# First two experts: the last 128 slots as a tile of their own, 448 columns and 64 rows behind a branch

## The chip, the cores and the metric

One core of a Trainium2 chip runs the whole kernel. Its engines have instruction streams of their own and wait for each other by semaphores: TensorE (PE in the profile; PEld is its weight loads) multiplies and transposes, VectorE (DVE) and ScalarE (ACT) work on tiles, GpSimd (POOL) issues the gathers and scatters here, and SyncE (SP) issues the other DMAs. The metric is the device time of one execution in microseconds, the median of several; the profile comes from one further execution.

## The reference

A linear attention with a complex decay gives x, and a mixture of eight experts follows. What matters here is the second part (x is 3072 tokens of 384, w1 is 8 x 384 x 1024, w2 is 8 x 1024 x 384):

```python
logits = x @ w_gate
noisy_logits = logits + np.log1p(np.exp(x @ w_noise)) * noise
top2 = np.argpartition(-noisy_logits, 2, axis=1)[:, :2]
...                                   # softmax over the two: top2_w
for e in range(E):
    for k in range(2):
        mask = top2[:, k] == e
        h = np.maximum(x[mask] @ w1[e], 0.0)
        out[mask] += top2_w[mask, k, None] * (h @ w2[e])
```

Each token goes to two of the eight experts, so an expert gets 768 tokens on average, some more and some fewer.

## The kernel before

The first 260 us compute the attention and the gates; a planner's table (ORDER) sets their order. Each token's row, with its gate weights and its number, is scattered to a slot of its expert in `xs`; an expert has 832 slots (CAP) that are computed, and two windows: window 0 and window 1. For the first two experts (not in TAILS) window 0 is slots 0 to 319 and window 1 is slots 320 to 831, both computed in full. For experts 2 to 7 (TAILS) window 1 is 512 slots, and window 0 is 256 slots and a tail of 64, slots 768 to 831.

For each window, SyncE loads its rows (`load_x`, into the single buffers `xga` for window 0 and `xgb` for window 1). `x_T` transposes them on TensorE, three blocks of 128 model columns (kk), each into one of two PSUM buffers `px`; ScalarE rounds each block to the high half and VectorE takes the low half. `mm1` makes eight groups of nine products (three blocks times high/high, high/low, low/high) of all the window's columns, each group into a buffer `ph`; ScalarE applies the Relu (`h`), VectorE takes the low half of `h`. `mm2_tile` then makes one tile of 128 slots from 24 products of 384 columns in `po`; for a tile of 64 slots it places the low half of `h` beside the high half as further rows and makes 16 products, and ScalarE and VectorE add the two halves of the result. VectorE scales the tile by the gate weight and adds it to the gathered rows `ao`, and GpSimd scatters them to `out`. The weights are split the same way as they arrive (`load_w1`, `load_w2`, a ring of three buffers `raw`).

Experts 2 to 7 branch already: `mm1_tail` loads a flag from `tail` (is the expert's count above 768?) on TensorE, VectorE, ScalarE and GpSimd. The long side runs window 0 with 320 columns and the 64-row tile, the short side with 256 columns and without that tile. SyncE doesn't take part.

The program's text from `mm2(0, 0)` on gives the work of the experts in the order in which it is written; the scheduler puts an engine's instructions in an order of their readiness, but what stands behind a branch in the text stays behind it on the engines that take it, apart from work that hangs on no instruction of the branch, which it may put ahead.

Of the kernel before, what the change touches and what calls it, by code (L numbers as in the profile page):

```python
# [9 lines left out]
F32 = mybir.dt.float32  # L10
# [3 lines left out]
I32 = mybir.dt.int32  # L14
# [63 lines left out]
def kernel(  # L78
# [460 lines left out]
    def load_x(e, w, dst):  # L539
        if w == 0:  # L540
            t = CAP - 64 if e in TAILS else 256
            ds = [nc.sync.dma_start(dst[:, 0:2], x3[e, 0:256].rearrange("(p j) r -> p j r", j=2)),
                  nc.sync.dma_start(dst[0:64, 2], x3[e, t:t + 64])]
            if e == 1:

                for d in ds:
                    for s in late:
                        tc.declare_no_dep(d.ins, s.ins, reason="slots behind the first 320")
        else:
            o = 256 if e in TAILS else 320  # L550
            nc.sync.dma_start(dst, x3[e, o:o + 512].rearrange("(p j) r -> p j r", j=4))

# [88 lines left out]
    def mm1_group(e, w, f, h, c):  # L643
        n = WIN[w][1]
        t = n % 128
        p = ps_tile("ph", 4)
        ms = [(i, j, kk) for kk in range(KD) for i, j in ((0, 0), (0, 1), (1, 0))]
        for m, (i, j, kk) in enumerate(ms):
            LAST['m'] = nc.tensor.matmul(p[:, :c], W1[e, kk][i][:, f * 128:(f + 1) * 128], XW[w, kk][:, j, 0:c],  # L649
                                         start=(m == 0), stop=(m == len(ms) - 1))  # L650
        nc.scalar.activation(h[:, 0:c], p[:, :c], AF.Relu)  # L651
        for dst, a, b in ((n + t, 0, n - t), (n, n - t, n)):
            b = min(b, c)
            if a < b:
                LAST['h'] = nc.vector.scalar_tensor_tensor(h[:, dst:dst + b - a], p[:, a:b], 0.0, h[:, a:b].bitcast(F32),  # L655
                                                           op0=OP.max, op1=OP.subtract)

    def mm1_tail(e):
# [8 lines left out]
        with cmp.Else():  # L667
            for f in range(KF):
                mm1_group(e, 0, f, hs[f], n - n % 128)

    def gather_o(e):
        for j in (2, 3, 4, 5, 6, 0, 1) if e in TAILS else range(7):
            w = TW[j]
            nc.gpsimd.indirect_dma_start(  # L674
                out=ao[j][0:w, :], out_offset=None, in_=out,
                in_offset=bass.IndirectOffsetOnAxis(ap=OX[e][0:w, j:j + 1], axis=0),
                bounds_check=N - 1, oob_is_err=False)
# [4 lines left out]

    def mm2(e, w):
        for j in JS[w]:
            if TW[j] == 128 or e not in TAILS:
                mm2_tile(e, w, j)

    def po_tile():
        return psO.tile([128, 512], F32, name="po")

    def mm2_tile(e, w, j, p=None):
        n, o = TW[j], 128 * (j - JS[w][0])
        p = p or po_tile()
        a, g = ao[j][0:n, :], GW[e][0:n, j:j + 1]
        if n == 128:
            ms = [(f, i, k2) for f in range(KF) for i, k2 in ((0, 0), (0, 1), (1, 0))]
            for m, (f, i, k2) in enumerate(ms):
                LAST['po'] = key(f"PO.{e}.{j}", nc.tensor.matmul(p[:, :DM], HT[w, f][i][:, o:o + 128], W2[f // 2][k2][:, f % 2, :],  # L698
                                                start=(m == 0), stop=(m == len(ms) - 1)))
        else:  # L700

            for f in range(KF):
                for k2 in range(2):
                    nc.tensor.matmul(p[0:2 * n, :DM], HT[w, f][0][:, o:o + 2 * n], W2[f // 2][k2][:, f % 2, :],  # L704
                                     start=(f == 0 and k2 == 0), stop=(f == KF - 1 and k2 == 1))
            lo = mt([n, DM], F32, name="lo")
            nc.scalar.copy(lo, p[n:2 * n, :DM])
            nc.vector.scalar_tensor_tensor(a, lo, g, a, op0=OP.mult, op1=OP.add)
        nc.vector.scalar_tensor_tensor(a, p[0:n, :DM], g, a, op0=OP.mult, op1=OP.add)  # L709
        d = nc.gpsimd.indirect_dma_start(  # L710
            out=out, out_offset=bass.IndirectOffsetOnAxis(ap=OX[e][0:n, j:j + 1], axis=0),
            in_=a, in_offset=None, bounds_check=N - 1, oob_is_err=False)
        if n == 128 and e in TAILS:

            for s in DONE.setdefault(e, []):
                tc.declare_no_dep(d.ins, s.ins, reason="rows differ")
            DONE[e].append(d)
# [125 lines left out]
    mm1(1, 0)  # L843
    x_T(0, 1)
    load_x(2, 0, xga)
    mm1(0, 1)
    load_x(1, 1, xgb)
    load_w1(2)
    mm2(0, 1)
# [1 line left out]

    lim = mp.tile([128, E], F32, name="lim")
    nc.gpsimd.iota(lim, pattern=[[N, E]], base=CAP, channel_multiplier=0, allow_small_or_imprecise_dtypes=True)

    for m in HALVES:
        nc.vector.tensor_add(bad[:, 0, 2 * m:2 * m + 1], bad[:, 0, 2 * m:2 * m + 1], bad[:, 0, 2 * m + 1:2 * m + 2])
# [1 line left out]
    nc.vector.tensor_scalar(decm, decm, DEC_MIN, None, op0=OP.is_lt)  # L860
    nc.vector.tensor_reduce(bad[0:112, 0, 1:2], decm[0:112], axis=AX.X, op=OP.max)
    nc.vector.tensor_scalar(bad[:, 1], bad[:, 1], TAN_MAX ** 2, None, op0=OP.is_gt)
    tail = cp.tile([1, E], I32, name="tail")
    nc.vector.scalar_tensor_tensor(tail, lim[0:1], -64.0, base_run[0:1], op0=OP.add, op1=OP.is_lt)
    few = mp.tile([128, E], F32, name="few")
    nc.vector.scalar_tensor_tensor(few, lim, float(FILL - CAP), base_run, op0=OP.add, op1=OP.is_gt)
    nc.vector.tensor_tensor(lim, base_run, lim, op=OP.is_gt)
# [13 lines left out]

    load_w2(1)
    gather_o(1)
    mm1(1, 1)
    load_x(2, 1, xgb)
    mm2(1, 1)
    x_T(2, 1)
# [185 lines left out]
```

## Time and profile before

| | |
|---|---|
| median of 3 runs | 709.2 us (709.17, 709.2, 710.77) |
| the profiled execution's own time | 710.01 us |
| its span | 708.3 us |
| mean granted clock of TensorE | 0.991 |
| busy in the span: PE, DVE, ACT, POOL | 94%, 58%, 46%, 24% |

The profile shows one execution. Its span is the time from the first to the last instruction; busy shares are over that span. A start time in a row is counted from the span's start. "Idle before" is how long an engine had nothing to do, and the arrow names what released it. The granted clock is a share of TensorE's full 2.4 GHz.

### The profile page before, as it was taken

How to read it: one execution, taken by the hardware profiler on the slowest of the kernel's cores; microseconds unless marked ns; L12 is line 12 of the kernel's file. 1: busy time of each engine (PE TensorE's matmuls, PEld its weight loads, DVE VectorE, ACT ScalarE, POOL GpSimd, SP SyncE). 2: the span in 40 equal slices, each digit the busy share in tenths (PEclk: the TensorE clock that was granted, in tenths of full speed). 3: DMA queues.
4: the chain of work that ended last, by engine and by line, in shares of the span. 5: the costliest groups of instructions: out<-in, count | busy, mean ns of one | idle time of the engine just before them, and what ended most of it. 6: DMA issues, size and time to landing. Idle time of an engine off the chain costs nothing.

```text
span 708.3 us, 13293 instructions
## 1 busy us (share of the span) xinstructions
PE 666.2 (94%) x5120; PEld 590.7 (83%) x5120; DVE 411.2 (58%) x919; ACT 328.0 (46%) x553; POOL 172.6 (24%) x183
## 2 busy tenths in 40 slices
PE   2599999999998999999999999999999999999995
PEld 0388887887776889898998998998999899899995
DVE  6799899999988747545237325425524524524311
ACT  7699888888775542324125215215313413413300
POOL 3000012451404225113224122322321411411311
PEclk9989999999999999999999999999999999999998
DMA  8877863654238516325128125425415515502201
GB/s 315 255 217 211 268 181 127 174 200 131 94 92 277 178 72 249 130 84 187 59 80 264 30 91 169 129 90 169 132 40 175 179 37 178 173 23 68 65 33 36
DMA packets 64190, 100.24 MB, mean 142 GB/s; under 512 B 26296, under 2 KB 46533, under 8 KB 64112
## 3 DMA queue, kind: packets, MB, share of 16 engines
q1 hardware_dynamic: 54752, 71.68, 32.7%
q0 software_dynamic: 9360, 27.54, 11.0%
q8 instruction: 46, 0.75, 0.4%
q14 instruction: 32, 0.26, 0.1%
HBM read 68.55 MB, written 31.69 MB: 142 GB/s over the span
## 4 chain that ended last, share of the span: by engine, by line
PE 80%; DVE 8%; ACT 5%; DMA 4%; issue 1%; SPq 1%; another core or an unknown queue 0%; POOL 0%; POOLq 0%; DVEq 0%; ACTq 0%
PE po L698 28%; PE ph L649 27%; PE ptr L354 4%; PE psc L363 4%; PE pY L412 2%; PE cum L307 2%; DMA raw<-in_moe_w_dram 2%; PE pY L414 2%; PE px L625 2%; PE pG L374 2%; PE po L704 2%; PE cum L331 1%; PE psc L649 1%; ACT t L248 1%; PE cum L427 1%
## 5 line engine op out<-in xcount | busy, mean ns | idle before, releaser
L698 PE MATMUL po<-w2h,h 128*128 128x384 f32 x768 | 203.9, 338 | 2.1 <-DVE ao L709 2.1
L649 PE MATMUL ph<-x,w1h 128*128 128x512 f32 (+2 forms) x720 | 187.2, 348 | 0.6 <-ACT x L630 0.5
L698 PEld LDWEIGHTS po<-w2h,h 128*128 128x128 f32 x768 | 139.4, 188 | 3.7 <-DVE ao L709 3.6
L649 PEld LDWEIGHTS ph<-x,w1h 128*128 128x128 f32 x720 | 125.7, 189 | 18.3 <-DVE h L655 1.3
L698 PE MATMUL po<-w2l,h 128*128 128x384 f32 x384 | 128.5, 335 | 0.0
L649 PE MATMUL ph<-x,w1l 128*128 128x512 f32 (+2 forms) x360 | 124.4, 347 | 0.0
L710 POOL DMA_INDIRECT out_dram<-ao,ox x52 | 50.9, 978 | 261.2 <-DVE ao L709 247.2
L497 POOL DMA_INDIRECT xs<-xr,sl x48 | 60.8, 1266 | 202.4 <-DVE qk L336 92.0
L655 DVE SCALAR_TENSOR_TENSOR h<-ph,h 128x512 fp32r<-128x512 f32 (+2 forms) x144 | 69.6, 505 | 67.5 <-ACT h L651 51.0
L651 ACT ACTIVATE h<-ph 128x512 fp32r<-128x512 f32 (+2 forms) x120 | 59.9, 507 | 102.0 <-PE ph L649 73.3
L709 DVE SCALAR_TENSOR_TENSOR ao<-po,gw,ao 128x384 f32<-128x384 f32 (+1 forms) x52 | 31.8, 614 | 125.1 <-PE po L698 124.8
L630 ACT CAST x<-px 128x512 fp32r<-128x512 f32 (+1 forms) x42 | 21.3, 518 | 125.5 <-PE px L625 125.5
L649 PEld LDWEIGHTS ph<-x,w1l 128*128 128x128 f32 x360 | 67.9, 189 | 7.9
L698 PEld LDWEIGHTS po<-w2l,h 128*128 128x128 f32 x384 | 72.2, 188 | 0.1
L674 POOL DMA_INDIRECT ao<-out_dram,ox x49 | 54.7, 1117 | 53.7 <-issue 31.7
L363 PE MATMUL psc<-qT,kT 112*128 112x128 f32 x384 | 54.1, 283 | 1.1 <-DVE h L655 0.6
L363 PEld LDWEIGHTS psc<-qT,kT 112*128 112x128 f32 x384 | 48.9, 196 | 5.9 <-issue 1.9
L586 ACT CAST w2h<-raw 128x768 fp32r<-128x768 f32 x32 | 26.5, 835 | 33.6 <-PE po L698 17.3
L414 PE MATMUL pY<-am,v 128*48 128x128 f32 x384 | 38.3, 275 | 1.6 <-DVE am L364 1.6
L587 DVE TENSOR_TENSOR w2l<-raw,w2h 128x768 fp32r<-128x768 f32 x32 | 30.4, 957 | 15.1 <-ACT w2h L586 14.2
L364 DVE TENSOR_TENSOR am<-psc,mask 128x512 f32<-128x512 f32 x48 | 32.8, 684 | 10.2 <-PE psc L363 8.6
L412 PE MATMUL pY<-qT,z 112*48 112x128 f32 x320 | 34.2, 279 | 0.2 <-DVE z L397 0.2
(211 smaller groups left out, 936.6 us busy)
## 6 DMA issues: line engine op xcount, KB each, us to landing
raw<-in_moe_w_dram SPq DMA_DIRECT2D x24, 512.0 KB
raw<-in_moe_w_dram SPq DMA_DIRECT2D x32, 384.0 KB
qk<-in_qk_dram SPq DMA_DIRECT2D x24, 384.0 KB
xgb<-xs SPq DMA_DIRECT2D x8, 800.0 KB
v<-in_v_dram SPq DMA_DIRECT2D x24, 192.0 KB
out_dram<-zero SPq DMA_DIRECT2D x12, 384.0 KB
re<-in_a_dram SPq DMA_DIRECT2D x11, 384.0 KB
im<-in_a_dram SPq DMA_DIRECT2D x11, 384.0 KB
```

Of the source, the lines that this page charges most:

```text
L363: key(f"P5{'ab'[half]}.{n}", nc.tensor.matmul(p[:, j, :], KT[n][:, h, :], QT[n][:, h, :], start=True, stop=True))
L364: LAST['am'] = nc.vector.tensor_mul(AM[n][:, 4 * half:4 * half + 4, :], p, mask[:, None, :].to_broadcast([128, 4, 128]))
L412: x = nc.tensor.matmul(o, Z[b][:, h, :], QT[n][:, h, :], start=True, stop=False, skip_group_check=True)
L414: x = nc.tensor.matmul(o, V[n][:, h, :], AM[n][:, h, :], start=not g, stop=True, skip_group_check=True)
L497: d = nc.gpsimd.indirect_dma_start(out=xs, out_offset=bass.IndirectOffsetOnAxis(ap=sl[:, kk, b:b + 1], axis=0), in_=XR[g][:, lo + b, :], i ...
L649: LAST['m'] = nc.tensor.matmul(p[:, :c], W1[e, kk][i][:, f * 128:(f + 1) * 128], XW[w, kk][:, j, 0:c], start=(m == 0), stop=(m == len(ms) ...
L651: nc.scalar.activation(h[:, 0:c], p[:, :c], AF.Relu)
L655: LAST['h'] = nc.vector.scalar_tensor_tensor(h[:, dst:dst + b - a], p[:, a:b], 0.0, h[:, a:b].bitcast(F32), op0=OP.max, op1=OP.subtract)
L674: nc.gpsimd.indirect_dma_start(out=ao[j][0:w, :], out_offset=None, in_=out, in_offset=bass.IndirectOffsetOnAxis(ap=OX[e][0:w, j:j + 1], ax ...
L698: LAST['po'] = key(f"PO.{e}.{j}", nc.tensor.matmul(p[:, :DM], HT[w, f][i][:, o:o + 128], W2[f // 2][k2][:, f % 2, :], start=(m == 0), stop ...
L709: nc.vector.scalar_tensor_tensor(a, p[0:n, :DM], g, a, op0=OP.mult, op1=OP.add)
L710: d = nc.gpsimd.indirect_dma_start(out=out, out_offset=bass.IndirectOffsetOnAxis(ap=OX[e][0:n, j:j + 1], axis=0), in_=a, in_offset=None, b ...
```

## The change

For experts 0 and 1 window 1 keeps its 512 columns, but its rows lie otherwise: 384 slots (320 to 703) are three tiles, and the last 128 slots (704 to 831) are a tile of their own, loaded by a second DMA. A branch on the same flag as before, `mm1_short`, takes the place of `mm1(e, 1)`: above 768 tokens it runs 512 columns and then the last tile with 128 rows; otherwise 448 columns and the last tile with 64. The last tile's second product is inside the branch, ahead of the other three. The flag's computation moves ahead of the first branch.

```diff
@@ -547,8 +547,10 @@
                     for s in late:
                         tc.declare_no_dep(d.ins, s.ins, reason="slots behind the first 320")
         else:
-            o = 256 if e in TAILS else 320
-            nc.sync.dma_start(dst, x3[e, o:o + 512].rearrange("(p j) r -> p j r", j=4))
+            o, m = (256, 4) if e in TAILS else (320, 3)
+            nc.sync.dma_start(dst[:, 0:m], x3[e, o:o + 128 * m].rearrange("(p j) r -> p j r", j=m))
+            if m == 3:
+                nc.sync.dma_start(dst[:, 3], x3[e, CAP - 128:CAP])
 
 
 
@@ -643,13 +645,15 @@
     def mm1_group(e, w, f, h, c):
         n = WIN[w][1]
         t = n % 128
+
+        to = ((n + t, 0, n - t), (n, n - t, n)) if w == 0 or c == n else ((n, 0, c - 64), (c, c - 64, c))
         p = ps_tile("ph", 4)
         ms = [(i, j, kk) for kk in range(KD) for i, j in ((0, 0), (0, 1), (1, 0))]
         for m, (i, j, kk) in enumerate(ms):
             LAST['m'] = nc.tensor.matmul(p[:, :c], W1[e, kk][i][:, f * 128:(f + 1) * 128], XW[w, kk][:, j, 0:c],
                                          start=(m == 0), stop=(m == len(ms) - 1))
         nc.scalar.activation(h[:, 0:c], p[:, :c], AF.Relu)
-        for dst, a, b in ((n + t, 0, n - t), (n, n - t, n)):
+        for dst, a, b in to:
             b = min(b, c)
             if a < b:
                 LAST['h'] = nc.vector.scalar_tensor_tensor(h[:, dst:dst + b - a], p[:, a:b], 0.0, h[:, a:b].bitcast(F32),
@@ -668,6 +672,20 @@
             for f in range(KF):
                 mm1_group(e, 0, f, hs[f], n - n % 128)
 
+    def mm1_short(e):
+        n = WIN[1][1]
+        hs = [h_tile(1, f) for f in range(KF)]
+        po = po_tile()
+        more = tail_value(e)
+        with tc.If(more > 0) as cmp:
+            for f in range(KF):
+                mm1_group(e, 1, f, hs[f], n)
+            mm2_tile(e, 1, 6, po)
+        with cmp.Else():
+            for f in range(KF):
+                mm1_group(e, 1, f, hs[f], n - 64)
+            mm2_tile(e, 1, 6, po, 64)
+
     def gather_o(e):
         for j in (2, 3, 4, 5, 6, 0, 1) if e in TAILS else range(7):
             w = TW[j]
@@ -682,14 +700,14 @@
 
     def mm2(e, w):
         for j in JS[w]:
-            if TW[j] == 128 or e not in TAILS:
+            if TW[j] == 128 and j < 6 or e not in TAILS and w == 0:
                 mm2_tile(e, w, j)
 
     def po_tile():
         return psO.tile([128, 512], F32, name="po")
 
-    def mm2_tile(e, w, j, p=None):
-        n, o = TW[j], 128 * (j - JS[w][0])
+    def mm2_tile(e, w, j, p=None, n=None):
+        n, o = n or TW[j], 128 * (j - JS[w][0])
         p = p or po_tile()
         a, g = ao[j][0:n, :], GW[e][0:n, j:j + 1]
         if n == 128:
@@ -843,7 +861,11 @@
     mm1(1, 0)
     x_T(0, 1)
     load_x(2, 0, xga)
-    mm1(0, 1)
+    lim = mp.tile([128, E], F32, name="lim")
+    nc.gpsimd.iota(lim, pattern=[[N, E]], base=CAP, channel_multiplier=0, allow_small_or_imprecise_dtypes=True)
+    tail = cp.tile([1, E], I32, name="tail")
+    nc.vector.scalar_tensor_tensor(tail, lim[0:1], -64.0, base_run[0:1], op0=OP.add, op1=OP.is_lt)
+    mm1_short(0)
     load_x(1, 1, xgb)
     load_w1(2)
     mm2(0, 1)
@@ -851,8 +873,6 @@
 
 
 
-    lim = mp.tile([128, E], F32, name="lim")
-    nc.gpsimd.iota(lim, pattern=[[N, E]], base=CAP, channel_multiplier=0, allow_small_or_imprecise_dtypes=True)
 
     for m in HALVES:
         nc.vector.tensor_add(bad[:, 0, 2 * m:2 * m + 1], bad[:, 0, 2 * m:2 * m + 1], bad[:, 0, 2 * m + 1:2 * m + 2])
@@ -860,8 +880,6 @@
     nc.vector.tensor_scalar(decm, decm, DEC_MIN, None, op0=OP.is_lt)
     nc.vector.tensor_reduce(bad[0:112, 0, 1:2], decm[0:112], axis=AX.X, op=OP.max)
     nc.vector.tensor_scalar(bad[:, 1], bad[:, 1], TAN_MAX ** 2, None, op0=OP.is_gt)
-    tail = cp.tile([1, E], I32, name="tail")
-    nc.vector.scalar_tensor_tensor(tail, lim[0:1], -64.0, base_run[0:1], op0=OP.add, op1=OP.is_lt)
     few = mp.tile([128, E], F32, name="few")
     nc.vector.scalar_tensor_tensor(few, lim, float(FILL - CAP), base_run, op0=OP.add, op1=OP.is_gt)
     nc.vector.tensor_tensor(lim, base_run, lim, op=OP.is_gt)
@@ -881,7 +899,7 @@
 
     load_w2(1)
     gather_o(1)
-    mm1(1, 1)
+    mm1_short(1)
     load_x(2, 1, xgb)
     mm2(1, 1)
     x_T(2, 1)
```

How this moves instructions is seen at three places. In these rows `px<-ident,xgb` is a transpose of window 1's rows, `ph<-x,w1h` (or w1l) a first product, `po<-w2h,h` a second one; the names behind "waits" are the semaphores, DMAHW those of SyncE's DMAs.

TensorE at expert 0's window 1, before: the window's twelve transposes (three blocks of four) and the first products of the window.

```order
L625 MATMUL px<-ident,xgb 128x128 [waits DMAHW2_49]
L625 MATMUL px<-ident,xgb 128x128 x3
L625 MATMUL px<-ident,xgb 128x128 [waits PE_49]
L625 MATMUL px<-ident,xgb 128x128 x3
L649 MATMUL ph<-x_3890,w1h_2720 128x512 [waits DVE_49,Activation_49]
L649 MATMUL ph<-x_3890,w1h_2720 128x512 [waits DVE_49] x2
L625 MATMUL px<-ident,xgb 128x128 [waits DVE_49]
L625 MATMUL px<-ident,xgb 128x128 x3
L649 MATMUL ph<-x_3890,w1h_2720 128x512
L649 MATMUL ph<-x_3890,w1l_2721 128x512
L649 MATMUL ph<-x_3898,w1h_2726 128x512 [waits Activation_49]
```

The same place after; `TENSOR_LOAD tail` and the branch are new.

```order
L627 MATMUL px<-ident,xgb 128x128 [waits DMAHW2_49]
L627 MATMUL px<-ident,xgb 128x128 x2
L627 MATMUL px<-ident,xgb 128x128 [waits DMAHW3_49]
L627 MATMUL px<-ident,xgb 128x128 [waits PE_49]
L627 MATMUL px<-ident,xgb 128x128 x3
L627 MATMUL px<-ident,xgb 128x128 [waits DVE_49]
L627 MATMUL px<-ident,xgb 128x128 x3
L698 TENSOR_LOAD tail [waits DVE_49]
L680 COMPARE_AND_BRANCH
L653 MATMUL ph<-x_3891,w1h_2720 128x512 [waits Activation_49]
L653 MATMUL ph<-x_3891,w1h_2720 128x512
```

The third block's transposes stood behind three products before; now all twelve stand ahead of the branch, and every first product behind it. In the first block the fourth transpose waits for the second DMA.

TensorE at expert 1's window 1, before: its twelve transposes (L625), the product of the flag (L878), and the first products.

```order
L625 MATMUL px<-ident,xgb 128x128 [waits DMAHW3_49,PE_49]
L625 MATMUL px<-ident,xgb 128x128 x3
L625 MATMUL px<-ident,xgb 128x128 [waits PE_49]
L625 MATMUL px<-ident,xgb 128x128 x3
L649 MATMUL ph<-x_4157,w1h_3517 128x512 [waits Activation_49]
L649 MATMUL ph<-x_4157,w1h_3517 128x512 x3
L625 MATMUL px<-ident,xgb 128x128 [waits DVE_49]
L625 MATMUL px<-ident,xgb 128x128 x3
L878 MATMUL px<-flg,ones_f 1x2 [waits DVE_49]
L649 MATMUL ph<-x_4157,w1h_3517 128x512
L649 MATMUL ph<-x_4157,w1l_3518 128x512
```

The same place after. Expert 1's first eight transposes stand 77 rows earlier, behind expert 0's branch; here are its last four (rows 1 and 2), the flag's product, and then eight transposes of expert 2's window 1, whose load is the one of SyncE with 1600 columns below.

```order
L627 MATMUL px<-ident,xgb 128x128 [waits PE_49]
L627 MATMUL px<-ident,xgb 128x128 x3
L896 MATMUL px<-flg,ones_f 1x2 [waits PE_49]
L627 MATMUL px<-ident,xgb 128x128 [waits DMAHW3_49,DVE_49]
L627 MATMUL px<-ident,xgb 128x128 x3
L627 MATMUL px<-ident,xgb 128x128 [waits DVE_49]
L627 MATMUL px<-ident,xgb 128x128 x3
L698 TENSOR_LOAD tail
L680 COMPARE_AND_BRANCH
L653 MATMUL ph<-x_4297,w1h_3517 128x512 [waits Activation_49]
L653 MATMUL ph<-x_4297,w1h_3517 128x512
```

Expert 2's transposes stood behind all of expert 1's second products of window 1 before; eight of them stand ahead of expert 1's branch now.

SyncE over the same stretch, before: the loads of window 1 for experts 0, 1 and 2 (xgb), and of weights (raw).

```order
L551 DMA xgb<-xs 128x1600 [waits DVE_49,Pool_49]
L551 DMA xgb<-xs 128x1600 [waits DMAHW2_49,DMAHW3_49,DVE_49,PE_49]
L603 DMA raw<-in_moe_w_dram 128x2x384 [waits DMAHW4_49,DVE_49]
L603 DMA raw<-in_moe_w_dram 128x2x384 [waits DMAHW5_49,DVE_49]
L603 DMA raw<-in_moe_w_dram 128x2x384 [waits DMAHW6_49,DVE_49]
L603 DMA raw<-in_moe_w_dram 128x2x384 [waits DMAHW7_49,DMAHW4_49,DVE_49]
L603 DMA raw<-in_moe_w_dram 128x2x384 [waits DMAHW5_49,DMAHW0_49,DVE_49]
L603 DMA raw<-in_moe_w_dram 128x2x384 [waits DMAHW6_49,DMAHW1_49,DVE_49]
L551 DMA xgb<-xs 128x1600 [waits DMAHW3_49,PE_49]
L603 DMA raw<-in_moe_w_dram 128x2x384 [waits DMAHW7_49,DVE_49]
```

After: experts 0 and 1 have two loads each (1200 and 400 columns), expert 2 has one (1600).

```order
L551 DMA xgb<-xs 128x1200 [waits DVE_49,Pool_49]
L553 DMA xgb<-xs 128x400 [waits DMAHW3_49]
L551 DMA xgb<-xs 128x1200 [waits DMAHW2_49,DMAHW4_49,DVE_49,PE_49]
L680 UNCONDITIONAL_BRANCH
L553 DMA xgb<-xs 128x400 [waits DMAHW5_49,DMAHW3_49,PE_49]
L605 DMA raw<-in_moe_w_dram 128x2x384 [waits DMAHW6_49,DVE_49]
L605 DMA raw<-in_moe_w_dram 128x2x384 [waits DMAHW7_49,DVE_49]
L605 DMA raw<-in_moe_w_dram 128x2x384 [waits DMAHW0_49,DVE_49]
L605 DMA raw<-in_moe_w_dram 128x2x384 [waits DMAHW6_49,DMAHW1_49,DVE_49]
L605 DMA raw<-in_moe_w_dram 128x2x384 [waits DMAHW7_49,DVE_49]
L551 DMA xgb<-xs 128x1600 [waits DMAHW5_49,DMAHW4_49,PE_49]
L605 DMA raw<-in_moe_w_dram 128x2x384 [waits DMAHW0_49,DVE_49]
```

Two DMAs are added; expert 2's load stands behind five weight loads instead of six, and still waits for TensorE's last transposes of expert 1.

## Rows read from the trace of the kernel before

**Rows 1.** The page: busy time by engine, and the chain's shares by engine.

```profile
PE 666.2 (94%) x5120; PEld 590.7 (83%) x5120; DVE 411.2 (58%) x919; ACT 328.0 (46%) x553; POOL 172.6 (24%) x183
...
PE 80%; DVE 8%; ACT 5%; DMA 4%; issue 1%; SPq 1%; another core or an unknown queue 0%; POOL 0%; POOLq 0%; DVEq 0%; ACTq 0%
```

**Rows 2.** The chain in order of time: start, length, engine, tile, line, count.

```profile
275.63 5.27 PE ph L649 x36
...
280.90 2.80 PE po L704 x16
...
291.49 16.13 PE ph L649 x69
...
307.62 16.65 PE po L698 x96
...
324.27 0.45 PE px L625 x4
...
327.14 15.81 PE ph L649 x68
...
342.95 16.67 PE po L698 x96
...
359.61 0.87 PE px L625 x8
```

**Rows 3.** TensorE's groups by shape: operands, count, busy us, mean ns.

```profile
L649 PE MATMUL ph<-x,w1h 128*128 128x256 f32 x192 | 34.6, 282 | 0.0
...
L649 PE MATMUL ph<-x,w1h 128*128 128x320 f32 x144 | 31.7, 309 | 0.0
```

**Rows 4.** TensorE over time, at window 1's transposes of experts 0 and 1.

```profile
288.81 1.03 PE L625 MATMUL px<-ident,xgb 128*128 128x128 f32 x8
290.09 0.97 PE L649 MATMUL ph<-x,w1h 128*128 128x512 f32 x3 [0.24 <-ACT x L630]
290.89 0.60 PE L625 MATMUL px<-ident,xgb 128*128 128x128 f32 x4
...
326.42 0.60 PE L625 MATMUL px<-ident,xgb 128*128 128x128 f32 x4
```

**Rows 5.** TensorE, then ScalarE, over time at expert 3's branch to the short side.

```profile
447.53 0.39 PE L649 MATMUL ph<-x,w1l 128*128 128x512 f32 x1
447.76 0.40 PE L649 MATMUL ph<-x,w1h 128*128 128x256 f32 x2
...
449.18 0.38 ACT L651 ACTIVATE h<-ph 128x256 fp32r<-128x256 f32 x1 [0.62 <-issue]
```

**Rows 6.** SyncE's waits from 280 to 293, then its DMAs over time.

```profile
SPq L551 <- DMA xgb<-xs: 6.1, 1, 6.1
...
282.03 9.81 SPq L551 DMA_DIRECT2D xgb<-xs  x2
...
327.05 0.34 SPq L551 DMA_DIRECT2D xgb<-xs  x1
```

**Rows 7.** VectorE over time: the flag, and the loads of experts 1 and 2 landing.

```profile
281.46 0.15 DVE L864 SCALAR_TENSOR_TENSOR tail<-lim,base_run 1x8 int32<-1x8 f32 x1 [3.14 <-POOL lim L855]
...
296.54 0.16 DVE L615 COPY gw<-xgb 128x4 f32<-128x4 f32 x1
...
333.09 0.17 DVE L615 COPY gw<-xgb 128x4 f32<-128x4 f32 x1 [1.72 <-DMA xgb<-xs]
```

**Rows 8.** TensorE over time, around its longest idle behind the start.

```profile
28.56 0.93 PE L374 MATMUL pG<-v,kh 128*48 128x48 f32 x32
34.86 1.96 PE L354 MATMUL ptr<-ident,qh 128*112 128x128 f32 x8 [5.38 <-ACT kT L355]
```

**Rows 9.** Windows: length, busy PE, PEld, DVE, ACT, POOL, granted clock, DMA, GB/s.

```profile
33.00:34.00 1.00, 0.00 (x0) 0.00 (x0) 0.07 (x1) 1.00 (x4) 0.00 (x0) 0.86 0.12 2
34.00:35.00 1.00, 0.14 (x1) 0.14 (x2) 0.96 (x2) 1.00 (x2) 0.00 (x0) 0.50 0.43 3
...
40.00:41.00 1.00, 1.00 (x9) 1.00 (x8) 1.00 (x3) 0.99 (x1) 0.00 (x0) 0.73 0.76 97
```

**Rows 10.** The page: the queue of TensorE's instruction fetches.

```profile
q8 instruction: 46, 0.75, 0.4%
```

## The prediction

> **What bounds the kernel now.** I read the page first: TensorE is busy for 94% of the span and carries 80% of the chain that ended last [rows 1]. I then read that chain in order of time over the stretch that the diff touches, from the first matmuls of expert 1 to the second half of its output. There it is TensorE almost alone: 36 products of 320 columns, the 64-row tile, 69 products of 512 columns, 96 products for four tiles, and so on, each group starting where the last one ended [rows 2]. So a column removed from TensorE here is time removed, and a TensorE wait added here is time added. After this stretch TensorE stays full to its last product, so nothing later takes either back.
>
> **Which side of the branch is taken.** The short side runs for 768 tokens or less. Counting the reference's top two on its own inputs (seed 0) gives 767 tokens for expert 0, 794 for expert 1, and above 768 among the others only experts 2 (774) and 4 (804). The trace agrees where it can: a run of this form holds 48 products with the high half of the weights; there are 192 of 256 columns, so four of the six old branches were short, and 144 of 320 columns, expert 1's first window and two long branches [rows 3]. So only expert 0 saves; expert 1 takes the branch and does all its old work.
>
> **The change part by part.**
>
> *First products, expert 0: 72 of 448 columns for 72 of 512.* A 512-column product costs 16.13/69 = 0.234 us, a 320-column one 5.27/36 = 0.146 us [rows 2]. That is 0.087 us over 192 columns, 0.029 us for 64; times 72: -2.10 us.
>
> *Second products, expert 0, last tile: 16 for 24.* 24 at 16.65/96 = 0.173 us are 4.16 us; the same 64-row form ran its 16 in 2.80 us [rows 2]: -1.36 us. Its extra copy and add are on ScalarE and VectorE, beside 72 products of the next three tiles: nothing. If that cover went they would cost about 1 us at the end only.
>
> *The branch itself, expert 0.* TensorE must issue its register load and jump behind all twelve transposes of the window. Before, three products ran while the last four transposes waited for a free buffer [rows 4]; now they come behind the jump: 3 x 0.234 = +0.70 us. The load and jump: in the old branches TensorE's product spacing over a jump to the short side stayed 0.23 us, and ScalarE, with less queued, showed 0.62 us of idle [rows 5]. So 0 to 0.6 us; TensorE has four transposes still running, so I take the near end, +0.1. At expert 1's branch eight transposes cover it: nothing. VectorE, ScalarE and GpSimd make the jump too, but wait for TensorE's groups of about 2 us anyway.
>
> *The load of the second window in two DMAs.* SyncE issues one instruction more. The old load of expert 0's window was seen complete after a wait of 6.1 us from about 282.4, so at 288.5 [rows 6], and its transposes began at 288.81 without idle [rows 4]: 0.3 us of slack. Same bytes, one issue of 0.34 us later: 0 to +0.5, I take +0.1. Expert 1's load has over 10 us to spare.
>
> *What the branch moves on TensorE, expert 1.* This is the term that decides. In the new order eight transposes of expert **2**'s second window stand ahead of expert 1's branch, and the first waits for that window's load. The load goes into the same buffer (xgb) that expert 1's transposes have just read, so SyncE can issue it only when the last four of these are done. Before, those four stood among expert 1's first products, and expert 2's transposes stood 35 us later, at 359.61 [rows 2]: the load had all that time. Now nothing can be issued on TensorE between the load's issue and its landing: behind the waiting transpose stand the other seven, the register load, and everything else of expert 1. Price: call P the start of the last four transposes of expert 1. The load issued 0.63 us after that (326.42 to 327.05) [rows 6, 7]. VectorE, waiting for the same load, went on at 333.09, 6.04 us after the issue; expert 1's own load, issued at 282.03 + 9.81 - 0.34 = 291.50, was there when VectorE asked for it at 296.54, so it took 5.04 us at most [rows 6, 7]. Three weight loads had been issued ahead of the first, none shortly ahead of the second; now two stand close ahead and one close behind, so I take the middle, 5.5 us. TensorE then begins expert 2's transposes at P + 0.63 + 5.5 = P + 6.1, after an idle of about 5.5 us (four transposes and the flag's product fill 0.6 us); eight transposes take 0.87 us and 72 products 72 x 15.81/68 = 16.74 us [rows 2]: the end is at P + 23.75. Before, the same products ended 342.95 - 324.27 = 18.68 us after the first of all twelve transposes [rows 2]. The difference is +5.1 us (+4.6 or a little less to +5.6 by the two loads). Eight of expert 1's transposes move ahead of the last three tiles and eight of expert 2's leave 359.61: 0.87 us each way, nothing.
>
> *The clock after that idle.* The trace has one idle of this length: TensorE did nothing for 5.38 us before 34.86. The granted clock fell from full to half inside it, at about 33.7 (0.86 over that us), and came back at about 40.5 (0.73 over that us); from 34.86 on TensorE worked 5.7 us at 1.2 instead of 2.4 GHz, so it lost 2.8 us [rows 8, 9]. The new idle is as long, so I take +2.8 us; if the clock held, 0.
>
> *The rest.* The threshold row (iota and one comparison) was ready at 281.6 before [rows 7] and TensorE asks for it behind 290.89 [rows 4]: nothing. Among expert 0's scatters the last tile's goes first now; GpSimd still writes each as its tile ends, and nothing on TensorE waits for one here: nothing.
>
> Sum: -2.10 - 1.36 + 0.70 + 0.1 + 0.1 + 5.1 + 2.8 = **+5.3 us**. The profiled execution took 710.01 us (span 708.3), 0.8 us above the median of the runs. On the median, 709.2 + 5.3 = **714.5 us** (715.3 from the profiled execution's own time).
>
> A rule that speaks against the change: the Trainium skill, "Runtime: NRT & Kernel Launch", section "Instruction fetch mechanics", says that a taken jump to instructions that are not yet in the engine's buffer stops the engine for a fetch. At the old jumps the row shows no gap on TensorE [rows 5], but there it had queued products to run. This rule is the fourth rival.
>
> **The rivals.**
> 1. *The wait is there but the clock stays up*: 709.2 + 5.3 - 2.8 = 711.7 us. For it: only one row shows the drop. Against: that idle was within 0.2 us of this one.
> 2. *The wait is hidden* (the other side). Without the idle the clock stays, and the terms are -3.46 + 0.70 + 0.2 and, since transposes and products would follow each other, 0.6 + 0.87 + 16.74 - 18.68 = -0.5: 709.2 - 3.1 = 706.1 us, faster. For it: the reduction is real, and TensorE is the bound. Against: the load would have to land at once; each us of it after the issue costs a us, and the change breaks even at about 3.0 us (with the clock up), while the load itself took 6.04 and the emptier one some 5.
> 3. *Expert 0 takes the long side*, so the change does not shorten anything: the 3.46 us are not saved, 717.9 us. For it: 767 is two tokens from the long side, and the chip's arithmetic is not the reference's. Against: the four old branches on the short side are those of the count.
> 4. *The jump costs a fetch*, where only four transposes cover it. 46 instruction packets took 0.4% of 16 engines' span, 45 us, so 1.0 us each [rows 10]: 715.5 us. Against: ScalarE's whole jump fitted into 0.62 us.
>
> **How the numbers follow.** Forecast 0.67, with 713.0 to 716.0 for itself; rival 1: 0.15; rival 2: 0.06; rival 3: 0.05; rival 4: 0.07. A difference within 0.3% (2.1 us) can't be told from no change. Rival 2 is the faster side, 0.06; the low end of rival 1 (a landing after 5.04 us gives 711.2, without the 0.2 for jump and split load 711.0) is within the bound, so same gets 0.07; slower 0.87. The range: the low end is rival 1 with a load a little quicker than 5.04 us, 710.8 us; the high end is the forecast with the slower load (+0.5), 0.5 for the jump and 0.4 for the split load, 715.9, and part of rival 3: 716.6 us.
>
> **What would show it.** In the profile after: an idle of 5 to 6 us on TensorE just ahead of expert 1's first products of 512 columns, released by a DMA into xgb, near 323; the granted clock at 0.5 for some us behind it; 72 products of 448 columns at about 0.205 us each and 16 products more at the 64-row line; no idle over 0.6 us at expert 0's jump. The prediction is wrong if that idle is under 3 us, if the clock stays at 1.0, or if no 448-column products are there.

## The result and the profile after

| | before | after |
|---|---|---|
| median | 709.48 us (708.61 to 710.77, 6 runs) | 716.6 us (714.04 to 718.08, 6 runs) |
| profiled execution, its span | 710.01, 708.3 us | 717.55, 715.8 us |

The ratio is 1.0096, with an interval of 1.0074 to 1.0118: slower by 7.1 us, where 5.3 were forecast. The time lies on the high end of the range (716.6), above the forecast's own 713.0 to 716.0.

The page's busy line answers to [rows 1]; the second line is TensorE's groups by shape, the new form.

```profile
PE 665.2 (93%) x5112; PEld 591.5 (83%) x5112; DVE 411.8 (58%) x928; ACT 328.3 (46%) x554; POOL 177.1 (25%) x183
...
L653 PE MATMUL ph<-x,w1h 128*128 128x448 f32 x48 | 13.9, 370 | 0.5 <-issue 0.5
```

TensorE has about the same busy time in a span that is 7.5 us longer; it has eight instructions less because expert 0 took the short side (16 second products for 24; its first products, 48 with the high half of the weights and 24 with the low half, have 448 columns). So the time went into waiting or a lower clock. TensorE over time at expert 0's and expert 1's windows shows where; the bracket is the idle time before the row. It answers to [rows 4].

```profile
288.26 1.03 PE L627 MATMUL px<-ident,xgb 128*128 128x128 f32 x8
290.28 0.66 PE L627 MATMUL px<-ident,xgb 128*128 128x128 f32 x4 [0.98 <-DVE x L633]
291.39 0.65 PE L653 MATMUL ph<-x,w1h 128*128 128x448 f32 x2 [0.46 <-issue]
...
322.51 0.60 PE L627 MATMUL px<-ident,xgb 128*128 128x128 f32 x4
323.03 0.19 PE L896 MATMUL px<-flg,ones_f 128*1 128x2 f32 x2
330.66 1.94 PE L627 MATMUL px<-ident,xgb 128*128 128x128 f32 x8 [7.43 <-DMA xgb<-xs]
332.25 1.20 PE L653 MATMUL ph<-x,w1h 128*128 128x512 f32 x2
...
334.96 1.05 PE L653 MATMUL ph<-x,w1h 128*128 128x512 f32 x2
...
336.14 0.63 PE L653 MATMUL ph<-x,w1h 128*128 128x512 f32 x2
```

The idle of 7.43 us is the forecast one, at the forecast place and with the forecast releaser. Behind it two products take 1.05 us instead of 0.63, until 336. In SyncE's row the load is issued 0.62 us after the last four transposes of expert 1 start, as worked out ([rows 6] has 0.63); it lands 7.5 us later.

```profile
323.13 0.34 SPq L551 DMA_DIRECT2D xgb<-xs  x1
```

The jumps' own records on TensorE, expert 0's to the short side and then expert 1's into the long side (shortest, median and longest ns, then the start):

```profile
L680 PEldq COMPARE_BRANCH  x1: 358/358/358, 290.9 to 290.9; - x1
L680 PEldq COMPARE_BRANCH  x1: 70/70/70, 331.1 to 331.1; - x1
```

Windows of 1 us (length, busy PE, PEld, DVE, ACT, POOL, granted clock, DMA share, GB/s):

```profile
325.00:326.00 1.00, 0.00 (x0) 0.00 (x0) 0.25 (x1) 0.71 (x1) 0.00 (x0) 0.89 0.77 224
326.00:327.00 1.00, 0.00 (x0) 0.00 (x0) 0.70 (x1) 0.00 (x0) 0.00 (x0) 0.50 1.00 307
...
335.00:336.00 1.00, 1.00 (x4) 0.81 (x3) 0.00 (x0) 0.00 (x0) 0.71 (x1) 0.50 0.30 65
336.00:337.00 1.00, 1.00 (x6) 0.83 (x5) 0.00 (x0) 0.53 (x1) 0.69 (x2) 0.99 0.39 149
```

The granted clock fell to 1.2 GHz inside the idle and came back at 336.0, as it did in [rows 9]: 5.35 us of work at half rate. The DMA share, the last column but one, shows the transfer engines nearly full while the load is under way.

By stages, from the start of expert 0's window-1 transposes (288.81 before, 288.26 after) to expert 2's first products (372.58 and 379.22) the kernel lost 7.19 us. From there to expert 7's first products (648.76 and 657.11) it lost 1.71 more: at three places TensorE waited for VectorE's `h`, 1.75 us in all, where the kernel before waited 0.15. It began the stretch 0.55 earlier, and its end was 0.8 shorter: 7.5 us in all. The chain view is of no use for this: in the kernel after it runs along GpSimd's scatters and "issue" for most of its length and gives TensorE 13%.

VectorE over time in the same stretch shows a second wait that the prediction put at nothing:

```profile
324.60 0.15 DVE L617 COPY gw<-xga 128x3 f32<-128x3 f32 x1
...
333.80 0.17 DVE L618 CAST ox<-xga 128x3 uint32<-128x3 f32 x1 [7.09 <-DMA out_dram<-ao,ox]
333.88 0.16 DVE L617 COPY gw<-xgb 128x4 f32<-128x4 f32 x1
...
337.18 0.69 DVE L659 SCALAR_TENSOR_TENSOR h<-ph,h 128x512 fp32r<-128x512 f32 x1 [3.04 <-issue]
```

`ox` holds the token numbers that the scatters read. There are two buffers, so expert 2's copy must wait for the last scatter of expert 0, which has landed by 333.80. In the new order this copy stands ahead of VectorE's jump at expert 1, so no `h` of expert 1 can pass it. Here TensorE is late anyway, and the wait stays hidden.

The scatter is late itself. GpSimd over time, the last two scatters of expert 0 after the change:

```profile
323.33 1.02 POOL L728 DMA_INDIRECT out_dram<-ao,ox  x1 [2.35 <-DVE w2l L589]
331.10 0.97 POOL L728 DMA_INDIRECT out_dram<-ao,ox  x1 [6.75 <-issue]
```

And the last one before:

```profile
325.90 0.97 POOL L710 DMA_INDIRECT out_dram<-ao,ox  x1 [3.88 <-DVE ao L709]
```

Before, the last scatter began 0.3 us after VectorE had finished its tile (325.63). After, the tile was finished at 324.02 and its scatter began 7.1 us later: GpSimd's queue waited, until 330.37, for the semaphore of the scatter of 323.33, so each scatter waits for the landing of the one ahead of it, and this landing took 7.0 us. (Before, the same wait had ended by 323.6, 2.6 us behind the scatter of 321.04.) The load of `xgb` and weight loads were under way at that time; that they made it late is likely and not shown.

### The profile page after: what moved, and what is told of

It reads as the page before. It is cut to its first block, busy times and chain, and to the rows that moved or that the text cites. A ratio compares the mean times of both kernels' runs of the same rounds, so it can differ in the third digit from the quotient of the medians.

```text
span 715.8 us, 13313 instructions
## 1 busy us (share of the span) xinstructions
PE 665.2 (93%) x5112; PEld 591.5 (83%) x5112; DVE 411.8 (58%) x928; ACT 328.3 (46%) x554; POOL 177.1 (25%) x183
## 5 line engine op out<-in xcount | busy, mean ns | idle before, releaser
L716 PE MATMUL po<-w2h,h 128*128 128x384 f32 x752 | 200.1, 339 | 2.1 <-DVE ao L727 2.1
L653 PE MATMUL ph<-x,w1h 128*128 128x512 f32 (+3 forms) x720 | 186.9, 348 | 2.2 <-DVE h L659 1.7
L716 PEld LDWEIGHTS po<-w2h,h 128*128 128x128 f32 x752 | 136.6, 188 | 3.6 <-DVE ao L727 3.6
L716 PE MATMUL po<-w2l,h 128*128 128x384 f32 x376 | 126.4, 336 | 0.0
L653 PE MATMUL ph<-x,w1l 128*128 128x512 f32 (+3 forms) x360 | 124.7, 346 | 0.0
L728 POOL DMA_INDIRECT out_dram<-ao,ox x52 | 54.1, 1041 | 271.8 <-DVE ao L727 226.9
L659 DVE SCALAR_TENSOR_TENSOR h<-ph,h 128x256 fp32r<-128x256 f32 (+3 forms) x152 | 69.7, 484 | 74.6 <-ACT h L655 58.6
L655 ACT ACTIVATE h<-ph 128x512 fp32r<-128x512 f32 (+3 forms) x120 | 59.5, 505 | 112.2 <-PE ph L653 90.3
L716 PEld LDWEIGHTS po<-w2l,h 128*128 128x128 f32 x376 | 70.7, 188 | 0.0
```

The costliest lines, as they stand in the source:

```text
L728: d = nc.gpsimd.indirect_dma_start(out=out, out_offset=bass.IndirectOffsetOnAxis(ap=OX[e][0:n, j:j + 1], axis=0), in_=a, in_offset=None, b ...
```

## The experiments

Two theories stood at first: the load of `xgb` that TensorE waits for costs all of it (with the clock behind it), or the branches themselves cost. Each kernel below has its own edit of the changed kernel, or of the kernel before, and was timed beside the kernel before on the same chip.

### One branch alone, and the wait taken away

**e1_expert0_only**: the branch at expert 0 alone.

```diff
-    mm1_short(1)
+    mm1(1, 1)
...                  # mm2 makes expert 1's last tile again, as before
```

> The changed kernel with the branch at expert 0 alone; expert 1 runs its 512 columns and its last tile of 128 rows without a branch, as before. If the loss is the wait of expert 2's transposes ahead of expert 1's branch (and the slow clock behind it), it is gone, and what stays is expert 0's part as the profile of the changed kernel shows it: -1.9 us (448 for 512 columns), -1.4 us (16 products for 24), +0.7 us (three products no longer under the transposes), +0.7 us (the jump's idle): about 707.6 us. Rival, the branches cost as such (flag load, jump, fetch): one of the two is left, so about half of the +7 stays, about 712 us.

Measured: 708.95 us, ratio 1.0002 (0.999 to 1.0015). The loss is gone with the second branch, but the gain isn't there: the time is 1.3 us above the expected 707.6. Its trace shows 0.98 us of this: TensorE waits for VectorE inside expert 1's products, since VectorE stands at that copy until 333.80:

```profile
334.62 0.73 PE L653 MATMUL ph<-x,w1h 128*128 128x512 f32 x2 [0.98 <-DVE h L659]
```

**e2_behind**: both branches, expert 2's transposes held behind expert 1's second products.

```diff
-    x_T(2, 1)
+    x_T(2, 1, last="po")
```

> The changed kernel, both branches kept; expert 2's transposes of window 1 are ordered behind the last product of expert 1's window 1 (one added ordering on TensorE). If TensorE's own wait for the load is the whole loss: no idle ahead of expert 1's products, clock 1.0, about 707.6 us. Rival, the branch costs as such: about 716 us as in the changed kernel. Second rival, VectorE's queue: its copies of expert 2's slot numbers still stand ahead of VectorE's jump and wait until about 11 us behind the last transposes for the load and for expert 0's scatters; TensorE fills its four buffers in about 9 us and then waits 2 to 4 us for VectorE: 709.5 to 711.5 us.

Measured: 714.78 us, ratio 1.0085 (1.0065 to 1.0105). A miss for the first theory: TensorE no longer waits for the load, and 5.8 of the 7.1 us are still there. TensorE over time in that trace:

```profile
336.71 0.73 PE L653 MATMUL ph<-x,w1h 128*128 128x512 f32 x2 [3.95 <-DVE h L659]
```

VectorE over time, what that `h` waited for:

```profile
335.31 0.17 DVE L618 CAST ox<-xga 128x3 uint32<-128x3 f32 x1 [7.55 <-DMA out_dram<-ao,ox]
...
335.96 2.48 DVE L659 SCALAR_TENSOR_TENSOR h<-ph,h 128x512 fp32r<-128x512 f32 x4 [0.32 <-issue]
```

And its windows of 1 us, the granted clock being the last column but two:

```profile
337.00:338.00 1.00, 1.00 (x6) 0.78 (x6) 1.00 (x3) 0.00 (x0) 0.80 (x1) 1.00 0.64 172
338.00:339.00 1.00, 1.00 (x4) 0.81 (x3) 0.45 (x1) 0.00 (x0) 0.89 (x1) 0.52 0.54 140
...
341.00:342.00 1.00, 1.00 (x5) 0.81 (x4) 0.23 (x1) 0.00 (x0) 0.70 (x2) 0.78 0.66 194
```

The hidden wait has come out; it is the second rival of the expectation. VectorE does four `h` at once at 335.96: four accumulators were full, and TensorE could not begin a fifth group. The 3.95 us are in the expected 2 to 4, but the time is 3.3 us above that rival's range: the idle costs the clock as well, from 338 to past 341 (0.48 + 0.5 + 0.5 + 0.22 = 1.7 us), and the later experts took 1.0 us more than before; the rest was not traced. So VectorE's queue ahead of its jump is a wait of its own, about 5.6 us here (3.95 and 1.7), and in the changed kernel the load's wait covered it.

**e3_own_buffer**: expert 2's window in a buffer of its own, so that its load needn't wait for expert 1's transposes. The transposes stay ahead of the branch.

```diff
+    xgc = mp.tile([128, 4, ROW], F32, name="xgc")
...                  # x_T reads expert 2's window 1 from xgc
-    load_x(2, 1, xgb)
+    load_x(2, 1, xgc)
```

> The changed kernel; expert 2's window 1 is loaded into a buffer of its own, so its load can be issued early, while its transposes stay ahead of expert 1's branch as in the changed kernel. If the loss is the wait for the load behind the buffer's release: the transposes run without idle, 707.5 to 708.5 us. If the loss is the place of the transposes, or the branch as such: about 716 us, with the idle still there.

Measured: 709.47 us, ratio 1.0013 (0.9993 to 1.0033). The load's wait is gone:

```profile
324.37 1.09 PE L627 MATMUL px<-ident,xgc 128*128 128x128 f32 x8 [1.45 <-DVE flag L899]
...
333.81 0.50 PE L653 MATMUL ph<-x,w1h 128*128 128x512 f32 x1 [0.15 <-DVE h L659]
```

VectorE still waits for the scatter here, but only to 332.44, and TensorE, itself held 1.45 us for its `px` buffer, meets that wait with 0.15 us only. So neither the branches nor the place of the transposes cost the 7 us. The time is 1.0 us above the expected 708.5 all the same: by the traces the stretch from expert 0's transposes to expert 2 is 0.9 us shorter than in the kernel before, and the later experts take 2.2 us more, again in waits for `h`.

**e4_busy**: 32 products whose result nobody reads fill the idle.

```diff
+    for m in range(32):
+        LAST['d'] = nc.tensor.matmul(pd, W1[1, 0][0][:, 0:128], XW[1, 0][:, 0, 0:512], start=(m == 0), stop=(m == 31))
...                  # behind the flag's product; expert 2's transposes behind these
```

> The changed kernel with 32 products of 512 columns (7.3 us, their result is not used) on TensorE behind the flag's product and ahead of expert 2's transposes, where it was idle for 7.4 us. If the half clock behind the idle costs time by itself: granted clock 1.0 throughout, 2.6 us less than the changed kernel, about 714 us. If the clock costs nothing that is not hidden: about 716.6 us.

Measured: 715.44 us, ratio 1.0084 (1.0061 to 1.0106). The clock stayed up, and the transposes, which the edit puts behind the fill, began as late as in the changed kernel:

```profile
322.62 0.60 PE L627 MATMUL px<-ident,xgb 128*128 128x128 f32 x4
...
323.27 7.57 PE L902 MATMUL po<-x,w1h 128*128 128x512 f32 x32
330.69 1.03 PE L627 MATMUL px<-ident,xgb 128*128 128x128 f32 x8
331.48 0.71 PE L653 MATMUL ph<-x,w1h 128*128 128x512 f32 x2
...
347.90 0.34 PE L716 MATMUL po<-w2h,h 128*128 128x384 f32 x1
```

From expert 0's transposes to expert 2's products it took 88.33 us, against 90.96 in the changed kernel: the clock is worth 2.6 us, near the forecast's 2.8. In its later experts TensorE waited longer for `h` (1.2 us more than the changed kernel lost there), so the median shows only part of it.

### The wait without a branch, and the landing

**e5_wait_alone**: the kernel before, no branch, with eight of expert 2's transposes ahead of expert 1's products (`early_T`; each product of `mm1(1, 1)` is kept behind them).

```diff
-    mm1(1, 1)
     load_x(2, 1, xgb)
+    early_T()
+    mm1(1, 1)
...                  # early_T itself, and the order behind it
```

> The kernel before, with no branch at either expert, but with eight of expert 2's twelve transposes put ahead of expert 1's first products, as the changed kernel has them. If TensorE's wait for the load of xgb is what costs and the branch has no part in it: an idle of 5.5 to 7.5 us ahead of the third group of transposes, half clock behind it (2.7 us), so 709.0 + 6.5 + 2.7 = 718, between 716 and 720. If the branch itself (its jump, its flag, its second queue entries) makes the loss: within 2 us of the kernel before, 709 to 711.

Measured: 718.73 us, ratio 1.0134 (1.0114 to 1.0154).

```profile
334.35 1.94 PE L613 MATMUL px<-ident,xgb 128*128 128x128 f32 x8 [6.25 <-DMA xgb<-xs]
```

So the wait costs what the first theory says, with no branch at all: besides the 6.25 us its trace has 1.13 us of idle for a `px` buffer just ahead, and half clock to 338.0, 3.6 us of work or 1.8 us lost. The branch matters because it moves these transposes.

**e6_loads_later**: expert 2's second weights loaded only behind its first transposes.

```diff
+            if e == 2:
+                tc.add_manual_dep(d.ins, LAST['x21'].ins.name, later, reason="pace")
...                  # 'x21' is the fourth of expert 2's transposes
```

> The changed kernel, with the loads of expert 2's second weights held until TensorE has expert 2's first transposes behind it, so that fewer bytes move beside the load of xgb. If the 7.5 us from issue to landing are 5.5 us of a lone load and 2 us of sharing the transfer engines: landing 5 to 6 us behind the issue and 714.5 (713.5 to 715.5). If the load takes that long by itself: 7 us or more and 716.6 as the changed kernel.

Measured: 716.81 us, ratio 1.0108 (1.0092 to 1.0125). The load was issued at 323.54:

```profile
328.99 1.94 PE L629 MATMUL px<-ident,xgb 128*128 128x128 f32 x8 [5.36 <-DMA xgb<-xs]
```

TensorE had it after 5.45 us, so 2 us of the 7.5 came from the weight loads beside it, as expected. The time did not follow. In the profiled execution (715.46 us, the quickest of its five) expert 2 begins 2.6 us sooner after expert 0's transposes than in the changed kernel, yet the median is no lower. What the other executions lost was not seen.

### VectorE's queue

**e7_behind_three** is e2_behind with three buffers for `gw` and `ox`.

```diff
-            GW[e] = mt([128, 7], F32, name="gw", bufs=2)
-            OX[e] = mt([128, 7], U32, name="ox", bufs=2)
+            GW[e] = mt([128, 7], F32, name="gw", bufs=3)
+            OX[e] = mt([128, 7], U32, name="ox", bufs=3)
```

> As e2_behind (both branches, expert 2's transposes behind expert 1's second products), with three buffers in place of two for gw and ox, so that expert 2's copy into ox no longer waits for expert 0's last scatter. If VectorE's queue ahead of its jump is what held e2_behind: the 3.95 us of TensorE's wait for h and the half clock behind it (1.6 us) go, 714.8 - 5.6 = 709.2; the copies then wait for the load of xgb alone, landing about 331 us, which is before TensorE wants its fifth accumulator (332.7), so at most 1 us of it comes back: 708 to 710. If the wait moves to that load in full, or if the branch itself costs: 713 or more.

Measured: 705.43 us, ratio 0.9954 (0.9936 to 0.9971). VectorE over time:

```profile
284.97 0.16 DVE L618 CAST ox<-xga 128x3 uint32<-128x3 f32 x1
...
329.69 0.17 DVE L617 COPY gw<-xgb 128x4 f32<-128x4 f32 x1 [4.16 <-DMA xgb<-xs]
...
330.28 2.48 DVE L659 SCALAR_TENSOR_TENSOR h<-ph,h 128x512 fp32r<-128x512 f32 x4 [0.34 <-issue]
```

With the third buffer free, the scheduler put the copy of `ox` some 50 us earlier, and the next copies wait for the load alone. TensorE waits 0.3 us for `h` in all. The drop of 9.4 us is more than the 5.6 expected. By the traces 5.4 of it lie between expert 0's transposes and expert 2, and 1.8 in the later experts, whose short waits came from the same two buffers; that was not expected. Another 1.9 us lie ahead of all that: the transposes of expert 0 began at 287.65 against 289.59, with the same work before them; what made that is not shown.

**e8_expert0_three** is e1_expert0_only with the same edit.

> As e1_expert0_only (branch at expert 0 alone), with three buffers for gw and ox. In e1_expert0_only TensorE waits 0.98 us for h, which VectorE has behind the same copy into ox. If that copy's wait is the reason: 709.0 - 1.0 = 708.0, just faster than the kernel before. If the wait only moves to the load of xgb: 709.0, as e1_expert0_only.

Measured: 705.0 us, ratio 0.9942 (0.9927 to 0.9957): 4.0 us better than two buffers, where 1.0 was expected. The traces show 2.4 of it: 1.4 up to expert 2, 1.0 in the later experts. The execution profiled for e1 was itself 1.0 us quicker than its median.

**e9_before_three** is the kernel before with the same edit: is it the buffers alone?

> The kernel before (no branch at the first two experts) with three buffers for gw and ox in place of two. By the traces, its later experts lose 0.45, 0.3 and 0.1 us of their first products to VectorE's copies into ox, and nothing at expert 1: 708.2. Then the branch at expert 0 alone is worth 708.2 - 705.0 = 3.2 us. If the third buffer and not the branch made e8_expert0_three faster: 705.0 to 706.

Measured: 711.17 us, ratio 1.003 (1.0013 to 1.0047). A miss on either theory. The later experts gained 0.92 us as expected, but the scheduler put expert 2's copies so early that they waited for a load of their own, ahead of an `h`. VectorE over time:

```profile
283.97 0.17 DVE L615 COPY gw<-xga 128x3 f32<-128x3 f32 x1 [2.70 <-DMA xga<-xs]
```

TensorE, in want of that `h`:

```profile
284.74 0.53 PE L649 MATMUL ph<-x,w1h 128*128 128x320 f32 x2 [2.29 <-DVE h L655]
```

**e10_after_three** is the changed kernel with the same edit.

> The changed kernel with three buffers for gw and ox, its eight transposes still ahead of expert 1's branch. If TensorE's wait for the load of xgb is a cost of its own that the buffers do not touch: 705.4 (e7_behind_three) + 6.3 to 7.4 of idle + 2.7 of half clock = 714.4 to 715.5. If the late landing of that load came from the scatters that VectorE waited for: 710 or less.

Measured: 714.31 us, ratio 1.0076 (1.0054 to 1.0098). The wait for the load is independent of the buffers:

```profile
331.18 1.94 PE L627 MATMUL px<-ident,xgb 128*128 128x128 f32 x8 [7.60 <-DMA xgb<-xs]
```

The half clock behind it is not: its windows of 1 us show it ending at 334.8, after 3.6 us of work, where the changed kernel has 5.35 behind as long an idle.

```profile
334.00:335.00 1.00, 1.00 (x4) 0.76 (x4) 0.00 (x0) 0.00 (x0) 0.00 (x0) 0.59 0.25 91
```

**e11_before_three_behind** and **e12_expert0_three_behind** make the clean pair that e9 failed to be: three buffers, expert 2's copies behind expert 1's last `h`, without and with the branch at expert 0.

```diff
-            if (e, w) == (0, 1):
+            if (e, w) in ((0, 1), (2, 0), (2, 1)):
                 behind_of(gx, 'h')
...                  # and three buffers for gw and ox, as in e7
```

> The kernel before with three buffers for gw and ox, and expert 2's copies into them held behind expert 1's last low half of h, so that they can't stand ahead of expert 1's products as in e9_before_three (where TensorE waited 2.3 us). TensorE's order is that of the kernel before. If the branch at expert 0 is what made e8_expert0_three faster: 709.1 less the 0.9 us that the later experts gain = 708.2, some 3 us above e8_expert0_three. If the buffers and the place of the copies made it: 705 to 706.

> The same with the branch at expert 0 alone. The only difference from e11_before_three_behind is then the branch, so the difference of the two is its worth: the forecast terms -2.10 and -1.36, with +0.70 for the three products and the 0.6 us that the jump was seen to cost, give -2.2; the stages of e8_expert0_three give -2.9. So 705.0 to 706.0, as e8_expert0_three. If the branch is worth nothing here: within 1 us of e11_before_three_behind.

Measured: 708.69 us, ratio 0.9993 (0.9979 to 1.0007), and 704.96 us, ratio 0.9943 (0.9925 to 0.9961). So the branch at expert 0, with the split load and the earlier flag that come with it, is worth 3.7 us by the medians once nothing waits. The chain in order of time without the branch (it answers to [rows 2]):

```profile
291.42 16.15 PE ph L649 x69
...
307.57 16.66 PE po L698 x96
```

And with it:

```profile
291.45 14.80 PE ph L653 x72
...
306.25 2.79 PE po L722 x16
...
309.92 12.49 PE po L716 x72
```

From expert 0's transposes to expert 7's first products the branch saves 358.80 - 356.12 = 2.68 us; this is what the traces show of its work. Most of the rest lies behind the last scatter's start: 7.6 us to the end of the span in one, 6.5 in the other. In the ten kernels with a new branch this stretch is 6.2 to 6.8 us, in the four without 6.9 to 7.6. What makes it is open.

## Why the prediction was right or wrong, point by point

Right in direction, place and mechanism; sizes were off, and two things that were put at nothing were wrong.

- *Which side is taken*: right; products of 448 columns for expert 0, 512 for expert 1.
- *First products* (-2.10): 72 in 14.96 us, 0.208 us each, against 0.234 [rows 2], is -1.9. *Last tile* (-1.36): 2.78 + 12.49 against 16.65 is -1.38 (the 12.49 from e12, where the same three tiles ran).
- *The branch at expert 0* (+0.70 and +0.1): mis-sized. The products began 3.13 us after the window's first transpose; before, the other 69 began at 2.44 [rows 4]. So 0.69 in place of 0.1: 0.46 of idle, which the trace calls issue, and a start that no longer overlaps the last transposes. (The idle of 0.98 us ahead of these is where the three products ran before, the +0.70.) The bound of 0.6 for the idle held. By the fourth rival 1.0 us was due, if the queue of [rows 10] is TensorE's, which the page does not say; TensorE shows 0.46. The rule of the Trainium skill named there (Runtime: NRT & Kernel Launch, "Instruction fetch mechanics") may be part of this idle: TensorE's record of the jump is 0.36 us here and 0.07 us at expert 1's branch, which went on into the long side. Whether the difference is a fetch, no row tells.
- *Load in two DMAs* (+0.1): nothing in this trace; the transposes began at 288.26 without idle.
- *The wait for the load* (+5.1): the mechanism was right, as e3, e5 and e10 show; the size was 6.6. By e4, at full clock, it is 25.3 us from P (322.62) to the end of the products (347.90), where 23.75 were worked out. The landing was mis-sized, 7.5 us for 5.5: it was taken as the middle of two landings, of which the one beside weight loads took 6.04. e6 shows the 2 us: 5.45 us when the loads of expert 2's second weights are held back.
- *The clock* (+2.8): 2.6 by e4. Rival 1 is out. That the size came so near is luck: it was taken from one row, and half clock lasted only 3.6 us in e5 and e10, 1.8 us lost. With the sizes so far the sum is -1.9 - 1.38 + 0.70 + 0.69 + 6.6 + 2.6 = +7.3; the stretch lost 7.19.
- *Rival 2* priced the kernel without any idle at 706.1 us; e7 gives 705.4, but that agreement is in part luck. By its trace e7 gained 2.3 us up to expert 2, where the terms say 3.1; the rest lies in the later experts (0.85, the third buffer), at the end and ahead of the stretch, where no term is. And the condition was wrong: taking the load's wait away leaves 714.8 (e2).
- *The step that failed*: "VectorE, ScalarE and GpSimd make the jump too, but wait for TensorE's groups of about 2 us anyway". VectorE had expert 2's copies queued ahead of its jump, one behind a scatter and one behind a load. I asked the question of what stands queued ahead of the jump on TensorE alone. "GpSimd still writes each as its tile ends, and nothing on TensorE waits for one here" fell with it, in both halves: the last scatter began 7.1 us behind its tile, and through VectorE TensorE waits for it (e1, e2). In the changed kernel the mistake cost nothing at expert 1, since the longer wait covers it; with that gone it is 5.6 us (e2).
- *The rest*: 1.71 us lost in the later experts were in no term, and 0.8 us of a shorter end neither. The 1.71 come from the two buffers: with three, e10 takes 275.37 us from expert 2's first products to expert 7's, the changed kernel 277.89.
- *The range*: that it still holds 716.6 is in part luck. Its high end was made of a slower load, a dearer jump and split load and part of rival 3; what filled it was 1.5 us more of the wait, 0.6 more of the jump and the 1.71, less 1.4 us at both ends of the stretch.

So the two kernels in question are both beaten by the branch at expert 0 alone, with three buffers for `gw` and `ox`: 705.0 us. The 705.4 of e7, with both branches, can't be told from that.

## What to carry to other kernels

A branch is a fence in every engine's queue: before adding one, list for each engine that takes it what the scheduler has put ahead of the jump, and what the slowest of these waits for, and whether that will come later than it did. Two such waits can lie over each other, so that taking one away shows the other and not the gain; take away both before judging the change itself. A third buffer for two tiles of 28 bytes a partition was worth 4 us by the medians at one place (e8 against e1, 2.4 of it in the traces) and cost 1.8 us at another (e9), by where it let the scheduler put the copies.

## What the runs showed of the hardware

- One load of 800 KB from issue to TensorE's use: 5.45 us when the last weight load was issued 1.7 us ahead of it and the next one only when it was there (e6), 6.35 us (e5), 7.53 us (the changed kernel) and 7.69 us (e10) with weight loads issued close ahead of it and behind it.
- An idle of 3.95 us on TensorE (e2) brought half clock 1.3 us after work had begun again, not inside the idle; the one of 7.43 us brought it inside, at 325.8. With products in the gap (e4) the granted clock stayed at 1.00. Behind the idle, half clock lasted 5.35 us of work in the changed kernel and 3.6 us in e5 and e10.
- A jump out of a flag's comparison, by its own record in the changed kernel: on TensorE 0.36 us to the short side (expert 0) and 0.07 us into the long side (expert 1); on ScalarE and VectorE 0.04 to 0.07 us at both.
